# Reordering accumulating products and splitting operand preparation in a 3-stage attention and mixture-of-experts kernel

## The chip, the cores and the metric

One core of one Trainium2 chip runs the whole program. The metric is device time in microseconds of one execution, given as the median of several runs. Before: 1076.45 us, the median of 3 runs (1072.89 to 1079.51).

## The reference

Three stages follow one another, all in float32:

```python
x = attention(rmsnorm(q) * g_q, rmsnorm(k) * g_k, v)    # 4 x 12 heads, 448 x 64
e = argmax(x @ w_gate); gate = softmax(x @ w_gate)[e]    # 1792 tokens, 768 wide
x = gate * (relu(x @ w1[e]) @ w2[e])                     # 8 experts, 768 -> 1024 -> 768
a, b = x @ m_w1, x @ m_w2                                # 768 -> 1024
out = ((a * b) @ m_w3) @ m_wo                            # 1024 -> 1024 -> 768
```

The change touches the end of the expert stage and the stage that computes `a * b`.

## The kernel before, in words

Every float32 operand of a product is held as two float16 parts, an upper one (the value rounded) and a lower one (the rest). ScalarE writes the upper part, VectorE then subtracts it from the value to get the lower one; `split` (L920) does both for weights. `mm3` (L927) makes each product of three matmuls: upper times upper, lower times upper, upper times lower. `m_w3 @ m_wo` is multiplied out early, beside the attention.

**Experts** (`expert`, L972, loop at L1171). Expert r runs 8 hidden blocks (f phase, 144 matmuls) and 6 output blocks (d phase, 144 matmuls) on its tokens, 320 down to 192 of them. After each block `between(r)` (L1149) issues other work: `convert` splits weight blocks of the next expert (6 of `w1`, 8 of `w2`), `stage` (L1072) issues the next weight load into one of four buffers on SP's queue, `ask` and `turn_rows` fetch the next tokens. Also there: at r = 1 one step of `extras` (L791), a table for tokens beyond an expert's capacity, whose rest runs just before expert 3; `overflow` (L1016) then reads its count `nxi` into registers of all engines and branches. At r = 3 to 5, seven steps of `operands(0)` (L1034); at r = 6 and 7, the first calls of `first_weights` (L1138).

**The last products** (`half`, L1248). `a` and `b` are computed by a 2 x 2 block scheme with seven products in place of eight. The activations are cut in two halves of columns, s = 0 (2 x 384) and s = 1 (2 x 512); `operands(s)` forms seven operands of each (B11, B21, B22 and four differences T1 to T4). The weights come in pieces (fp, z, j): output blocks fp = 0 to 3, matrix z = 0 or 1 (`m_w1` or `m_w2`), row blocks j = 0 to 2. A piece is turned from 64-bit to 32-bit floats (`from64`, L204: three VectorE instructions), four sums are formed (L1122 to L1125), and it is split (L1130). `half(fp, s)` runs, for z = 0 and 1, seven products of 9 matmuls each (3 blocks j, 3 matmuls each), in this order, with the PSUM bank and what reads it:

- A11*B11 starts a bank; ScalarE copies it out (`u`, L1290). A12*B21 adds to the same bank, read again (L1294 or L1298).
- S2*T2 starts a bank; VectorE adds it to `u`.
- S3*T3 starts a bank; VectorE makes `t1` from it. A22*T4 adds to the same bank; VectorE makes `x21`.
- S1*T1 starts a bank; VectorE adds it to `t1`. S4*B22 adds to the same bank; VectorE adds it to `u`.

So three of the seven products add to a bank whose first sum was read one instruction earlier. For z = 1 each result is multiplied with that of z = 0 (`finish`, L1278) and split into `ab` by ScalarE and GpSimd (`done`, L1273).

After each product `rest()` (L1268) calls `fill(slot, us)` (L1203): it adds the product's time, less that of its own VectorE read, to a credit (at most 2.5 us) and issues steps from the list `todo` while the credit is positive and the step's slot has come. In `todo` stand the seven steps of `operands(1)`, then sums and splits of the pieces of fp = 1 to 3. Sums run on VectorE for fp = 1, on GpSimd for fp = 2 and 3. `force` (L1211) issues what is still missing before a z begins. After `half(0, 0)` the rest of `operands(1)` is issued in one go (L1342).

Each engine works in the order in which its instructions are written: `flow.pin()` fixes that order for all of them. The last stage (L1364 on) multiplies `ab` by the prepared weights, with 672 matmuls.

Of the kernel before, what the change touches and what calls it, by code (L numbers as in the profile page):

```python
# [8 lines left out]
F32 = mybir.dt.float32  # L9
F16 = mybir.dt.float16  # L10
# [110 lines left out]
def fused_kernel(ctx, tc, q, k, v, g_q, g_k, w_gate, w1, w2, m_w1, m_w2, m_w3, m_wo, out):  # L121
# [831 lines left out]
    def bank(n):  # L953
        return mm_p.tile([P, 512], F32, tag="mm", name="psm")[:, 0:n]
# [79 lines left out]
    def operands(s):  # L1034

        c1, c2 = halves(s)
        b11, b21, b12, b22 = y32[:, 0:3, c1], y32[:, 3:6, c1], y32[:, 0:3, c2], y32[:, 3:6, c2]
        tt = nc.vector.tensor_tensor

        unit = 3 * PC[s][1] / 1000  # L1040

        def put(o, x):
# [3 lines left out]
        put(B11, b11)  # L1046
        yield 1.16 * unit
        put(B21, b21)
        yield 1.16 * unit
        put(B22, b22)  # L1050
        yield 1.16 * unit
# [7 lines left out]
        put(T3, b12)  # L1059
        yield 2.32 * unit  # L1060
        tt(b21, b21, b22, op=ALU.subtract)
        put(T4, b21)
        yield 2.32 * unit
# [47 lines left out]
    def stage_sums(item, home, e):  # L1111
# [8 lines left out]
        y = y.bitcast(F32)  # L1120
# [7 lines left out]
    wst2 = {}  # L1128

    def stage_split(item):  # L1130
        fp, z, j, y = item
        t = w1p.tile([P, 2, DF], F16, tag="w1", name="m2w")[:, :, 0:7 * P]
        split(t, y[:, 0:7].rearrange("p a b -> p (a b)"), 16.0)
        wst2.setdefault((fp, z), []).append(t)

    sums_ = []

    def first_weights():  # L1138
        if staged:
            k = staged[0][1] * 3 + staged[0][2]  # L1140
            sums_.append(stage_sums(staged.pop(0), xtp if k % 2 else ycv, nc.vector))
            stage()
        if len(sums_) > 1 or not staged:
            stage_split(sums_.pop(0))
# [4 lines left out]
    def between(r):  # L1149
        def go(i):  # L1150
# [4 lines left out]
            if r == 1:  # L1155
                next(excess, None)
# [25 lines left out]
    while sums_:  # L1182
        first_weights()
# [16 lines left out]
    todo, credit = [], 0.0  # L1200
    last_operand = None

    def fill(slot, us):  # L1203

        nonlocal credit
        credit = min(credit + us, 2.5)
        while todo and todo[0][0] <= slot and credit > 0:
            credit -= todo[0][1]()
            todo.pop(0)

    def force(key):  # L1211

        while len(wst2.get(key, ())) < 3:
            todo.pop(0)[1]()

    second = operands(1)
    for _ in range(7):
        todo.append((0, lambda: next(second)))
    ends = len(todo)
    pieces = [(fp, z, j) for fp in range(1, SB) for z in range(2) for j in range(3)]  # L1220
    loaded, summed = [], []

    def begin_loads(n=1):
        for _ in range(n):
            if pieces:
                loaded.append(stage_load(*pieces.pop(0), dst))

    def sums_step(e):
        def go():
            summed.append(stage_sums(loaded.pop(0), yst, e))  # L1230
            begin_loads()
            return 2.7 if e is nc.vector else 1.9
        return go

    def split_step():
        stage_split(summed.pop(0))
        return 1.1

    for i, (fp, z, j) in enumerate(pieces):
        gate = 28 * (fp - 1) + 22 * z if z or fp > 1 else 0  # L1240
        todo.append((gate, sums_step(nc.vector if fp == 1 else nc.gpsimd)))
        if i:
            todo.append((gate, split_step))
    todo.append((0, split_step))
    begin_loads(2)
    ab = []

    def half(fp, s):  # L1248
# [34 lines left out]
        later = []  # L1283
        for z in range(2):
            force((fp, z))
            w = wst2[fp, z]
            ps = bank(n)
            product(ps, w, A11, B11, True)
            u = temp("ub" if z else "ua", s)
            nc.scalar.activation(u, ps, AF.Copy, scale=1.0 if z else r)  # L1290
            rest()
            product(ps, w, A12, B21, False)
            if z:
                tt(a[0, 0], ps, a[0, 0], op=ALU.mult)  # L1294
                done(0, 0, a[0, 0])
            else:
                a[0, 0] = temp("a11", s)
                nc.scalar.activation(a[0, 0], ps, AF.Copy, scale=r)  # L1298
# [5 lines left out]
            ps = bank(n)  # L1304
            product(ps, w, S3, T3, True)
            t1 = temp("u3", s)
            add(t1, ps, u, z)
            rest()
            product(ps, w, A22, T4, False)
            x21 = temp("c21", s)  # L1310
            add(x21, ps, u, z)
            outs = [((1, 0), x21), ((1, 1), t1), ((0, 1), u)]

            def end(i):
                k, x = outs[i]
                if not z:
                    a[k] = x
                elif len(ab) == 1:
                    later.append((k, a[k], x))
                else:  # L1320
                    finish(k, a[k], x)

            end(0)
            rest()
            ps = bank(n)
            product(ps, w, S1, T1, True)
            add(t1, ps, t1, z)
            end(1)
            rest()
            product(ps, w, S4, B22, False)  # L1330
            add(u, ps, u, z)
            end(2)
# [6 lines left out]
    ab.append(ab0p.tile([P, 2, NT], F16, name="ab0"))  # L1339
    h = half(0, 0)  # L1340
    next(h)
    for _ in second:  # L1342
        pass
    while todo and todo[0][1].__name__ == "<lambda>":
        todo.pop(0)
# [12 lines left out]
    assert not todo  # L1358
# [42 lines left out]
```

## Time and profile before

| | us |
|---|---|
| median of 3 runs | 1076.45 |
| lowest, highest | 1072.89, 1079.51 |
| the profiled execution, its own time | 1066.05 |
| its span, first to last instruction | 1064.3 |
| attention and routing, to | 375.5 |
| experts, to | 654.5 |
| the products of `half`, to | 947.7 |
| last products and output, to | 1064.3 |

PE is TensorE, DVE VectorE, ACT ScalarE, POOL GpSimd, SP the queue that issues most loads. The times of stages are starts of PE's first matmuls in the profiled execution. In a timeline row the brackets give the idle time of the engine before the group and what ended it.

### The profile page before, as it was taken

The numbers are of one execution on the slowest core, as the hardware profiler recorded it, in microseconds if no ns is written. First come the engines' busy times: TensorE is split into PE (matmuls) and PEld (weight loads), VectorE is DVE, ScalarE is ACT, GpSimd is POOL, SyncE is SP. The second block draws the span as 40 slices with busy tenths as digits, with TensorE's granted clock in tenths as the row PEclk, the third lists the DMA queues.
The fourth block names the chain that finished last, engine by engine and source line by source line (L and its number), as shares of the span: only waits on it lengthen the run. The fifth ranks groups of instructions, "written<-read, shape, count | busy, mean of one in ns | idle before, by whom it ended". The sixth has DMA issues, their size and how long they took to land.

```text
span 1064.3 us, 19475 instructions
## 1 busy us (share of the span) xinstructions
PE 889.7 (84%) x7766; PEld 590.8 (56%) x7766; DVE 647.1 (61%) x959; ACT 478.5 (45%) x738; POOL 309.2 (29%) x317
## 2 busy tenths in 40 slices
PE   0588899999999899997998796757776877899997
PEld 0255566666666477885897795323332433446664
DVE  6898898788988633554656769646746644330000
ACT  4797788888784433453655554221212211110000
POOL 6275667767331251100010100010324322121111
PEclk9898899999999899998998898879899998999999
DMA  7767698875999857873895784102201101011111
GB/s 190 186 134 181 153 200 157 181 153 108 218 213 218 233 157 186 255 221 116 240 280 160 220 247 131 40 0 80 79 20 60 60 21 44 3 72 60 45 60 45
DMA packets 200350, 144.43 MB, mean 136 GB/s; under 512 B 139376, under 2 KB 178832, under 8 KB 200256
## 3 DMA queue, kind: packets, MB, share of 16 engines
q1 hardware_dynamic: 197248, 131.39, 48.0%
q0 software_dynamic: 3008, 11.76, 3.3%
q8 instruction: 62, 1.02, 0.4%
q14 instruction: 32, 0.26, 0.1%
HBM read 103.52 MB, written 14.18 MB: 111 GB/s over the span
## 4 chain that ended last, share of the span: by engine, by line
PE 29%; DVE 11%; DMA 5%; ACT 4%; issue 3%; SPq 1%; POOLq 0%; DVEq 0%; ACTq 0%
PE psm L933 20%; PE pso L1371 10%; DMA st<-in_moe_w_dram 4%; ACT b L1043 1%; DVE m2w L922 1%; DVE y32w L206 1%; DVE u L1266 1%; DVE w1t L922 1%; DVE y32w L207 1%; DVE u L1264 1%; DVE w2t L922 1%; DVE b L1044 1%; DMA xte<-xr 1%; DVE y32w L205 1%; SPq L950 1%
## 5 line engine op out<-in xcount | busy, mean ns | idle before, releaser
L933 PE MATMUL psm<-b,m2w 128*128 128x384 f16 (+1 forms) x1008 | 213.8, 370 | 79.4 <-DVE u L1264 28.0
L933 PEld LDWEIGHTS <-m2w 128*128 128x128 f16 x1008 | 102.1, 102 | 190.7 <-issue 104.9
L933 PEld LDWEIGHTS <-w1t 128*128 128x128 f16 x1152 | 111.6, 100 | 41.5 <-issue 9.3
L933 PE MATMUL psm<-xte,w1t 128*128 128x288 f16 (+6 forms) x1008 | 111.5, 274 | 22.6 <-PEq L1020 7.8
L933 PE MATMUL psm<-ht,w2t 128*128 128x320 f16 (+7 forms) x1152 | 125.4, 270 | 1.9 <-DVE w2t L922 1.9
L933 PEld LDWEIGHTS <-w2t 128*128 128x128 f16 x1152 | 108.8, 98 | 17.2 <-DVE w2t L922 2.9
L1371 PE MATMUL pso<-ww,ab 128*128 128x384 f16 x672 | 109.4, 326 | 0.0
L404 DVE TENSOR_REDUCE nm<-psm 128x2 f32<-128x896 f32 x84 | 88.6, 1084 | 11.5 <-PE psm L402 11.2
L461 PE MATMUL po<-vf,e 128*128 128x65 f32 (+1 forms) x576 | 89.7, 274 | 4.6 <-ACT w L227 4.6
L1371 PEld LDWEIGHTS <-ab 128*128 128x128 f16 x672 | 65.8, 98 | 43.6
L922 DVE SCALAR_TENSOR_TENSOR w1t<-st,w1t 128x1024 f16<-128x1024 f32 x42 | 51.2, 1224 | 56.5 <-ACT w1t L921 54.8
L461 PEld LDWEIGHTS po<-vf,e 128*128 128x128 f32 (+1 forms) x576 | 70.7, 179 | 20.3 <-issue 12.3
L402 PE MATMUL psm<-kt,qt 64*64 64x448 f16 x336 | 47.4, 380 | 37.9 <-DMA qt<-qf 28.2
L723 POOL DMA_INDIRECT xr<-xd,ix x19 | 23.3, 1226 | 191.0 <-DMA ix<-md 120.3
L431 PE MATMUL pss<-qt,kt 64*128 64x448 f16 (+1 forms) x576 | 67.8, 377 | 11.1 <-DVE e L446 10.0
L1375 DVE TENSOR_SCALAR ob<-pso,meta_s 128x384 f32<-128x384 f32 x14 | 8.6, 617 | 99.8 <-PE pso L1371 99.8
L1276 POOL TENSOR_TENSOR ab<-a,ab 128x384 f16<-128x384 f32 (+1 forms) x8 | 8.6, 1078 | 196.0 <-ACT ab L1275 196.0
L464 PE MATMUL po<-v,e 128*128 128x65 f16 (+1 forms) x480 | 63.9, 195 | 1.7 <-DVE lacc L525 1.7
L465 PE MATMUL po<-vl,e 128*128 128x64 f16 (+1 forms) x480 | 63.8, 194 | 0.0
L922 DVE SCALAR_TENSOR_TENSOR w2t<-st,w2t 128x768 f16<-128x768 f32 x56 | 52.9, 955 | 16.7 <-ACT w2t L921 15.6
L466 PE MATMUL po<-v,e 128*128 128x65 f16 (+1 forms) x480 | 63.0, 194 | 0.0
L446 DVE TENSOR_TENSOR e<-pss,e 128x896 f16<-128x896 f32 x48 | 51.6, 1083 | 7.1 <-ACT e L444 6.8
(256 smaller groups left out, 1636.9 us busy)
## 6 DMA issues: line engine op xcount, KB each, us to landing
st<-in_moe_w_dram SPq DMA_DIRECT2D x42, 512.0 KB, 5.4
st<-in_moe_w_dram SPq DMA_DIRECT2D x56, 384.0 KB, 4.1
st<-in_moe_w_dram SPq DMA_DIRECT2D x48, 256.0 KB, 3.3
w<-in_moe_w_dram SPq DMA_DIRECT2D x16, 512.0 KB, 4.9
w<-in_moe_w_out_dram SPq DMA_DIRECT2D x16, 384.0 KB, 3.7
xd<-rx SPq DMA_DIRECT2D x12, 448.0 KB, 4.6
kf<-in_k_dram SPq DMA_DIRECT2D x24, 192.0 KB, 2.9
qf<-in_q_dram SPq DMA_DIRECT2D x24, 192.0 KB, 3.3
```

What stands on the lines that cost most here:

```text
L402: nc.tensor.matmul(ps[h, z, 0:S], lhsT=s["q"][0][h, c:c + 64], rhs=s["k"][0][h, S * j:S * j + S], start=True, stop=True)
L404: nc.vector.tensor_reduce(s["nm"][:, t], ps[:, :, 0:S], axis=AX.X, op=ALU.max, negate=True)
L431: nc.tensor.matmul(ps[o, h, 0:S], lhsT=l, rhs=rt[HD[h], S * j:S * j + S], start=a == 0, stop=a == 3)
L446: nc.vector.tensor_tensor(lo, p, hi, op=ALU.subtract)
L461: nc.tensor.matmul(ov[r, t, :], lhsT=e[0], rhs=vfs[i % 2][:, h, c, 0:D + 1], start=z == 0, stop=z == 3)
L464: nc.tensor.matmul(ov[r, t, :], lhsT=e[0], rhs=vh, start=z == 0, stop=False)
L465: nc.tensor.matmul(ov[r, t, 0:D], lhsT=e[0], rhs=s["vl"][:, h, c, :], start=False, stop=False)
L466: nc.tensor.matmul(ov[r, t, :], lhsT=e[1], rhs=vh, start=False, stop=z == 3)
L723: nc.gpsimd.indirect_dma_start(out=dst, out_offset=None, in_=xd, in_offset=bass.IndirectOffsetOnAxis(ap=ix[0:dst.shape[0], t:t + 1], axis=0))
L922: nc.vector.scalar_tensor_tensor(dst[:, 1], src, scale, dst[:, 0], op0=ALU.mult, op1=ALU.subtract)
L933: nc.tensor.matmul(ps, lhsT=x, rhs=y, start=first and j == 0, stop=last and j == n - 1, **kw)
L1371: nc.tensor.matmul(pp[z], lhsT=ab[f][:, x, ts], rhs=ww[f][:, y, z * 384:(z + 1) * 384], start=f == 0 and x == 0 and y == 0, stop=f == 7 an ...
```

## The change

Three things. In `half` the products are reordered: A11*B11, S2*T2, S3*T3 and S1*T1 each start a bank, then A12*B21, A22*T4 and S4*B22 add to the first, third and fourth of them. `operands` and the making of weight pieces become generators in which ScalarE's upper part is issued one step ahead of VectorE's lower part, with one or two VectorE instructions in a step; `operands(0)` takes 12 steps, `operands(1)` 11. Four of the six pieces of fp = 0 are made between expert blocks (instead of all six before `half(0, 0)`), the other two within `half(0, 0)`, ahead of `operands(1)`; the middle pieces (j = 1) of fp = 1 get their sums on GpSimd. The steps of `extras` run at r = 1 and 2.

```diff
+        def hi(o, x):
             nc.scalar.activation(bt[s][o][:, 0], x, AF.Copy)
+        def lo(o, x):
             tt(bt[s][o][:, 1], x, bt[s][o][:, 0], op=ALU.subtract)
...
-        tt(b12, b12, b11, op=ALU.subtract)
-        put(T1, b12)
-        yield 2.32 * unit
-        tt(b22, b22, b12, op=ALU.subtract)
-        put(T2, b22)
-        yield 2.32 * unit
...
+        hi(T1, b12)
+        lo(B22, b22)
+        yield unit
         tt(b22, b22, b12, op=ALU.subtract)
+        yield unit
+        hi(T2, b22)
+        lo(T1, b12)
+        yield unit
         tt(b12, b22, b11, op=ALU.subtract)
+        yield unit
+        hi(T3, b12)
+        lo(T2, b22)
+        yield unit
         tt(b21, b21, b22, op=ALU.subtract)
+        yield unit
+        hi(T4, b21)
+        lo(T3, b12)
+        yield unit
+        lo(T4, b21)
+        yield unit
...
-    loads = [(r, k) for r in range(1, NE) for k in range(14)] + [(NE, k) for k in range(1, 6)]
-    loads.insert(loads.index((NE - 1, 6)), (NE, 0))
+    loads = [(r, k) for r in range(1, NE) for k in range(14)] + [(NE, k) for k in range(2, 4)]
+    for k in (0, 1):
+        loads.insert(loads.index((NE - 1, 6)), (NE, k))
...
+    def in_parts(n, blocks_, sums):
+
+        b, t = [], []
+        for k in range(n + 1):
+            if k:
+                t.append(stage_upper(b.pop(0)))
+            if k < n:
+                b.append(blocks_(k))
+                c = sums(b[-1])
+                yield k, 1.8 + c
+            if t:
+                stage_lower(t.pop(0))
+                yield k, 1.1
...
+    first_weights = in_parts(4, first_blocks, lambda b: stage_sums(b, nc.vector) and 1.15)
...
-            if r == 1:
+            if r in (1, 2):
                 next(excess, None)
...
-            if i in {LR: (9, 11), LR + 1: (9, 11, 13), LR + 2: (9, 11)}.get(r, ()):
+            if i in {LR: (8, 10, 12), LR + 1: (9, 10, 11, 12, 13), LR + 2: (9, 11, 12, 13)}.get(r, ()):
                 next(early)
-            if r == NE - 2 and i == 13 or r == NE - 1 and i in (8, 10, 12):
-                first_weights()
+            for _ in range({NE - 2: (0, 0, 0, 0, 1, 1), NE - 1: (1,) * 6}[r][i - 8] if i >= 8 and r >= NE - 2 else 0):
+                next(first_weights)
...
+    def steps():
+        second = operands(1)
+        pieces = [(0, 1, 1), (0, 1, 2)] + [(fp, z, j) for fp in range(1, SB) for z in range(2) for j in range(3)]
+        loaded = [stage_load(*x, dst) for x in pieces[:2]]
...
+            own_ = fp == 0 or fp == 1 and j != 1
+            stage_sums(b, nc.vector if own_ else nc.gpsimd)
...
+        for k, c in in_parts(2, blocks_, sums):
+            yield 0, c
+        for c in second:
+            yield 0, c
+        done2.append(True)
+        for k, c in in_parts(len(pieces) - 2, lambda k: blocks_(k + 2), sums):
+            fp, z, j = pieces[min(k + 2, len(pieces) - 1)]
+            yield 28 * (fp - 1) + 22 * z if z or fp > 1 else 0, c
...
+            p1 = bank(n)
+            product(p1, w, A11, B11, True)
             u = temp("ub" if z else "ua", s)
...
+            p4 = bank(n)
+            product(p4, w, S1, T1, True)
+            add(t1, p4, t1, z)
+            end(z, (1, 1), t1)
+            rest()
+            product(p1, w, A12, B21, False)
...
+            product(p3, w, A22, T4, False)
             x21 = temp("c21", s)
-            add(x21, ps, u, z)
...
+            add(x21, p3, u, z)
+            end(z, (1, 0), x21)
             rest()
...
+            product(p4, w, S4, B22, False)
+            add(u, p4, u, z)
+            end(z, (0, 1), u)
             rest()
...
-    for _ in second:
-        pass
-    while todo and todo[0][1].__name__ == "<lambda>":
-        todo.pop(0)
+    while not done2:
+        one()
     ylife.close()
```

## Rows read from the trace of the kernel before

**Rows 1.** Waits of PE, 654 to 948 us: total us, times, longest.
```profile
PE psm L933 <- DVE u L1264: 28.0, 16, 4.7
PE psm L933 <- ACT ua L1290: 27.3, 8, 11.1
PE psm L933 <- DVE u L1266: 14.6, 16, 2.4
PE psm L933 <- ACT ub L1290: 5.2, 8, 0.7
```

**Rows 2.** Windows: length; busy PE, PEld, DVE, ACT, POOL; clock; DMA share, GB/s.
```profile
654.50:709.50 55.00, 28.33 (x138) 14.65 (x136) 36.27 (x46) 16.92 (x19) 2.17 (x3) 0.79 0.06 20
709.50:749.80 40.30, 31.65 (x126) 13.12 (x126) 24.49 (x47) 6.47 (x10) 5.40 (x6) 0.90 0.16 53
749.80:783.80 34.00, 25.05 (x126) 12.94 (x126) 23.74 (x40) 6.84 (x12) 11.43 (x16) 0.90 0.24 78
...
947.70:1064.30 116.60, 109.16 (x672) 65.52 (x670) 10.09 (x16) 8.75 (x15) 15.71 (x16) 0.99 0.14 54
```

**Rows 3.** Timeline of PE in `half(3, 0)` and `half(3, 1)`, without filled-in work.
```profile
896.82 3.08 PE L933 MATMUL psm<-b,m2w 128*128 128x384 f16 x18 [0.65 <-DVE u L1266]
...
904.22 4.55 PE L933 MATMUL psm<-b,m2w 128*128 128x384 f16 x27 [0.58 <-ACT ub L1290]
...
917.52 5.99 PE L933 MATMUL psm<-b,m2w 128*128 128x512 f16 x27 [0.74 <-ACT ua L1290]
...
924.29 4.04 PE L933 MATMUL psm<-b,m2w 128*128 128x512 f16 x18 [0.78 <-DVE u L1266]
```

**Rows 4.** Timeline at the starts of `half(0, 0)` and `half(0, 1)`.
```profile
662.98 0.95 ACT L921 ACTIVATE m2w<-y32x 128x896 f16<-128x896 f32 x1 [2.90 <-DVE y32x L1125]
...
664.36 7.03 PE L933 MATMUL psm<-b,m2w 128*128 128x384 f16 x27 [7.67 <-ACT ua L1290]
...
709.51 8.10 PE L933 MATMUL psm<-b,m2w 128*128 128x512 f16 x27 [11.10 <-ACT ua L1290]
```

**Rows 5.** Timeline on DVE: one piece's sums begin, then a lower part.
```profile
656.17 0.43 DVE L205 TENSOR_SCALAR y32w<-st 128x512 uint32<-128x512 uint32 x1
...
659.02 1.08 DVE L922 SCALAR_TENSOR_TENSOR m2w<-y32x,m2w 128x896 f16<-128x896 f32 x1
```

**Rows 6.** Groups by line, 654 to 948 us: busy us, mean ns, idle before.
```profile
L1044 DVE TENSOR_TENSOR b<-y,b 128x1536 f16<-128x1536 f32 x7 | 12.3, 1758 | 8.8 <-ACT b L1043 8.8
L1266 DVE SCALAR_TENSOR_TENSOR ua<-psm,ua 128x384 f32<-128x384 f32 (+1 forms) x16 | 10.0, 624 | 36.9 <-PE psm L933 36.9
```

**Rows 7.** Timeline of `half(2, 1)`: a VectorE instruction alone, then one beside GpSimd.
```profile
870.02 0.69 DVE L206 SCALAR_TENSOR_TENSOR y32w<-st,y32w 128x512 uint32<-128x512 uint32 x1
...
870.39 1.33 POOL L1276 TENSOR_TENSOR ab<-a,ab 128x512 f16<-128x512 f32 x1 [19.80 <-ACT ab L1275]
870.74 1.53 DVE L207 SCALAR_TENSOR_TENSOR y32w<-st,y32w 128x512 uint32<-128x512 uint32 x1
```

**Rows 8.** Waits of PE in the experts, 375 to 655 us.
```profile
PE psm L933 <- PEq L1020: 7.8, 1, 7.8
PE psm L933 <- ACT w1t L921: 7.2, 3, 3.3
PE psm L933 <- DVE w1t L922: 5.3, 6, 1.0
```

**Rows 9.** Timeline in the experts: `extras`, a lower part, the last expert.
```profile
484.64 0.68 DVE L837 TENSOR_TENSOR xf<-xe,xs 128x512 f32<-128x512 f32 x1
...
487.93 0.15 DVE L844 CAST nxi<-xt 128x1 int32<-128x1 f32 x1
...
562.29 1.36 DVE L1044 TENSOR_TENSOR b<-y,b 128x1152 f16<-128x1152 f32 x1 [1.23 <-ACT b L1043]
...
630.76 0.43 DVE L205 TENSOR_SCALAR y32w<-st 128x512 uint32<-128x512 uint32 x1 [1.36 <-DMA st<-in_moe_w_dram]
...
644.26 10.41 PE L933 MATMUL psm<-ht,w2t 128*128 128x192 f16 x122 [0.55 <-DVE w2t L922]
```

More of the change, by code (lines that the diff above doesn't have):

```diff
@@ L1126, in stage_sums, with stage_upper, stage_lower, first_blocks @@
         return fp, z, j, y
-    wst2 = {}
-    def stage_split(item):
+    def stage_upper(item):
         fp, z, j, y = item
         t = w1p.tile([P, 2, DF], F16, tag="w1", name="m2w")[:, :, 0:7 * P]
-        split(t, y[:, 0:7].rearrange("p a b -> p (a b)"), 16.0)
-        wst2.setdefault((fp, z), []).append(t)
[L1136 to L1144, printed above, removed]
+        y = y[:, 0:7].rearrange("p a b -> p (a b)")
+        nc.scalar.activation(t[:, 0], y, AF.Copy, scale=16.0)
+        return fp, z, t, y
+    wst2 = {}
+    def stage_lower(item):
+        fp, z, t, y = item
+        nc.vector.scalar_tensor_tensor(t[:, 1], y, 16.0, t[:, 0], op0=ALU.mult, op1=ALU.subtract)
+        wst2.setdefault((fp, z), []).append(t)
+    def in_parts(n, blocks_, sums):
[10 more added lines that the diff above has]
+                yield k, 1.1
+    def first_blocks(k):
+        b = stage_blocks(staged.pop(0), xtp if k % 2 else ycv)
+        stage()
+        return b
+    first_weights = in_parts(4, first_blocks, lambda b: stage_sums(b, nc.vector) and 1.15)
     FC = {0: (0, 1, 0, 1, 0, 1, 0, 0), LR: (0, 1, 1, 2, 1, 1, 1, 1)}
@@ L1181, in fused_kernel @@
         pass
-    while sums_:
-        first_weights()
+    for _ in first_weights:
+        pass
     meta_s = const.tile([P, 2 * TP, 3], U32, name="meta_s")
@@ L1198, in temp, with one @@
         return w2p.tile([P, 2, DM], F16, tag="w2", name=name).rearrange("p a b -> p (a b)").bitcast(F32)[:, 0:PC[s][1]]
-    todo, credit = [], 0.0
-    last_operand = None
+    work, gate, credit = None, 0, 0.0
+    def one():
+        nonlocal gate
+        gate, c = next(work, (1000, 0))
+        return c
     def fill(slot, us):
@@ L1206, in fill, with blocks_, sums @@
         credit = min(credit + us, 2.5)
-        while todo and todo[0][0] <= slot and credit > 0:
-            credit -= todo[0][1]()
-            todo.pop(0)
+        while gate <= slot and credit > 0:
+            credit -= one()
     def force(key):
         while len(wst2.get(key, ())) < 3:
[L1214 to L1245, printed above, removed]
+            one()
+    done2 = []
+    def steps():
+        second = operands(1)
+        pieces = [(0, 1, 1), (0, 1, 2)] + [(fp, z, j) for fp in range(1, SB) for z in range(2) for j in range(3)]
+        loaded = [stage_load(*x, dst) for x in pieces[:2]]
+        def blocks_(k):
+            b = stage_blocks(loaded.pop(0), yst)
+            if k + 2 < len(pieces):
+                loaded.append(stage_load(*pieces[k + 2], dst))
+            return b
+        def sums(b):
+            fp, z, j, y = b
+            own_ = fp == 0 or fp == 1 and j != 1
+            stage_sums(b, nc.vector if own_ else nc.gpsimd)
+            return 1.15 if own_ else 0
+        for k, c in in_parts(2, blocks_, sums):
[6 more added lines that the diff above has]
+            yield 28 * (fp - 1) + 22 * z if z or fp > 1 else 0, c
+    ab = []
     ab = []
@@ L1283, in half, with end @@
         later = []
+        def end(z, k, x):
+            if not z:
+                a[k] = x
+            elif len(ab) == 1:
+                later.append((k, a[k], x))
+            else:
+                finish(k, a[k], x)
         for z in range(2):
@@ L1286, in half @@
             w = wst2[fp, z]
-            ps = bank(n)
-            product(ps, w, A11, B11, True)
+            p1 = bank(n)
+            product(p1, w, A11, B11, True)
             u = temp("ub" if z else "ua", s)
[L1290 to L1298, printed above, removed]
+            nc.scalar.activation(u, p1, AF.Copy, scale=1.0 if z else r)
             rest()
@@ L1303, in half @@
             rest()
-            ps = bank(n)
-            product(ps, w, S3, T3, True)
+            p3 = bank(n)
+            product(p3, w, S3, T3, True)
             t1 = temp("u3", s)
-            add(t1, ps, u, z)
+            add(t1, p3, u, z)
             rest()
-            product(ps, w, A22, T4, False)
-            x21 = temp("c21", s)
-            add(x21, ps, u, z)
[L1312 to L1323, printed above, removed]
-            rest()
[L1325 to L1332, printed above, removed]
+            p4 = bank(n)
[4 more added lines that the diff above has]
+            product(p1, w, A12, B21, False)
+            if z:
+                tt(a[0, 0], p1, a[0, 0], op=ALU.mult)
+                done(0, 0, a[0, 0])
+            else:
+                a[0, 0] = temp("a11", s)
+                nc.scalar.activation(a[0, 0], p1, AF.Copy, scale=r)
+            rest()
+            product(p3, w, A22, T4, False)
+            x21 = temp("c21", s)
+            add(x21, p3, u, z)
+            end(z, (1, 0), x21)
+            rest()
+            product(p4, w, S4, B22, False)
+            add(u, p4, u, z)
+            end(z, (0, 1), u)
             rest()
@@ L1339, in fused_kernel @@
     ab.append(ab0p.tile([P, 2, NT], F16, name="ab0"))
+    work = steps()
     h = half(0, 0)
     next(h)
-    for _ in second:
-        pass
-    while todo and todo[0][1].__name__ == "<lambda>":
-        todo.pop(0)
+    while not done2:
+        one()
     ylife.close()
@@ L1357, in fused_kernel @@
                     pass
-    assert not todo
+    assert next(work, None) is None
     prep2.close()
```

35 lines of the change are left out of this document (21 added, 14 removed).

## The prediction

> **What bounds the kernel now.** I read the page's busy shares first (PE 84%, DVE 61%), then the windows by stage, then PE's waits in the stages that the change touches, then the timeline there. The last stage is full (109 of 116.6 us busy at clock 0.99, [rows 2]) and stays as it is. The stage between, 654.5 to 947.7 us, takes 293.2 us. What PE needs for it at full clock follows from [rows 3]: a product of 9 matmuls takes 4.55 - 3.08 = 1.47 us with 384 columns and 5.99 - 4.04 = 1.95 us with 512. There are 56 of each (4 blocks, 2 matrices, 7 products): 82.3 + 109.2 = 191.5 us. The other 101.7 us are waits and slow matmuls. The four rows of [rows 1] add up to 75.1 us: 48 waits, one for each of the three adding products of a z, 16 times over. Where nothing else is queued, such a wait is 0.58 to 0.78 us [rows 3]; 48 of those would be about 33 us. The rest is engine order: the instruction that reads the bank stands behind filled-in work. At 664.36 PE had waited 7.67 us for ScalarE's copy, which stood behind splits that waited for VectorE's sums, and at 709.51 it had waited 11.10 us, behind `operands(1)` [rows 4]. After such waits the matmuls run slow (27 in 8.10 us where 5.99 is the full pace, [rows 3, 4]) and the granted clock of the first three windows is 0.79 to 0.90 [rows 2]. So of the 26.6 us that the waits leave over, most are slow matmuls.
>
> So the stage has two parts. Up to 783.8 us (`half(0, 0)`, `half(0, 1)`, `half(1, 0)`) VectorE is close to full: 36.3 + 24.5 + 23.7 = 84.5 us busy of 129.3 [rows 2], and PE's 20.6 + 27.3 + 20.6 = 68.5 us of work are less than that. From there to 947.7 us (163.9 us) PE's five halves need 123.1 us and VectorE has room.
>
> **Part by part.**
>
> 1. *Reordered products.* No instruction is added. An adding product now comes four products after its bank's start (A12*B21), three (A22*T4) or three (S4*B22), so the read has at least two whole products, 2.9 or 3.9 us, in which to finish, against an empty-queue cost of about 0.7. Four banks per z are open as before, of eight. In the second part this removes all waits that are not longer than the slack. A filled-in burst there is at most the credit of 2.5 us and one step more, some 3 to 4 us of VectorE, and the evictions behind it have two products of time: I leave 3 us for what sticks out. 123.1 + 3 = 126 against 163.9: **-38**. Bounds: 123 (nothing) and 138 (a wait of some 3 us left at each of five bursts), so -41 to -26.
>
> 2. *First part of the stage.* PE no longer waits for ScalarE's copy, so VectorE's chain decides. Its work: the two late pieces of fp = 0 at 659.02 - 656.17 + 1.08 = 3.9 us each [rows 5], 8; what is left of the third and fourth lower parts, 2.5; `operands(1)`, seven lower parts and four differences of the same size at 1.76 [rows 6], 19.5; reads and `finish`, 14 in each half at a mean of 0.62 [rows 6], 26; fp = 1, four pieces at 3.9 and two with sums on GpSimd at 3.0, 22; three of fp = 2, 9. That is 87 with each instruction at its full length. The busy time of before, in which neighbours overlap, was 84.5; it held some 2 us more of sums, which go to GpSimd now. I take 82.5. In front of it comes a new wait: the loads of the two late pieces go into buffers that lie where the earlier ones were, so they can only start at the end of the fourth lower part; 4.5 us from the first product is my value (0 if the memory is free earlier, 8 if all of it waits). Queued behind this wait on VectorE are the reads of S2*T2, S3*T3 and S1*T1; PE runs on until A22*T4, so it loses some 3 us there, and the chain already holds that. Small gaps, 4. Sum 91 against 129.3: **-38**. Bounds: 83 (-46) if it has no gap; 105 (-24) if half of VectorE's idle 44.8 us of before stays.
>
> 3. *Slow matmuls.* They go with the long pauses, and the terms above have them at full pace. `half(0, 1)` still begins after sparse work on PE; I give back 3 us (0 to 10; one such start cost 2.1 before, [rows 3, 4]): **+3**.
>
> 4. *`extras` earlier.* Seven VectorE instructions, 484.64 to 488.08, stood between the last weight of expert 3 and the count that all engines read; PE restarted 4.5 us later, after 7.8 us [rows 8, 9]. The 4.5 us of reading and branching stay. The seven move to expert 2's hidden blocks, beside its `w2` conversions, and I cost them there at nothing; if those conversions are late by them, the gain is gone. **-3.3**, bounds 0 and -7.8.
>
> 5. *`operands(0)` in steps.* In the put of before, VectorE sat 1.23 us at each T for ScalarE [rows 9], with conversions of `w1` behind it. PE's waits for those [rows 8] come to 12.5 us, nearly all at the starts of experts 5 and 6. One step ahead, ScalarE's part is done when VectorE needs it. But loads and ScalarE's conversion also arrive late there, so I take **-5**, bounds 0 and -11.9.
>
> 6. *Weight pieces earlier.* The second piece's load and sums now stand ahead of the eight `w2` conversions of the last expert, on SP's queue (512 KB) and on VectorE (2.85 us, and a wait for that load; the first piece already waited 1.36 us, [rows 9]). Behind them stand the hidden parts and those conversions, and PE needs all eight early in its d phase, where it waited at 644.26 [rows 9]. So PE starts later by about one piece: **+3.2**, bounds 0 and +7. It is paid back in term 2, where the remaining sums no longer stand in front of `half(0, 0)`.
>
> 7. *Sums of two pieces on GpSimd.* It has time. But [rows 7] show a VectorE instruction of two inputs at 1.53 us beside a GpSimd one, against 0.69. The Trainium skill (SBUF — State Buffer, SBUF: two separate sides) calls the shared pair of ports an exclusive lock: the later of the two waits the whole instruction out. The trace agrees with that here: 0.84 us more. By the lock, eight more GpSimd instructions could cost VectorE up to eight such delays, 6.7 us in the first part, in place of the 1.7 us that moving the sums saves; the sum would be 5 us higher. In it they stand at nothing, because most GpSimd rows of the kind fall beside work that is not delayed.
>
> Sum: -38 - 38 + 3 - 3.3 - 5 + 3.2 = **-78**. The profiled execution took 1066.05 us, 1.75 more than its span, so the changed kernel would take 988 of its kind. The runs' median stands 1.0% above that execution; scaled, 988 * 1076.45 / 1066.05 = **997 us**.
>
> **Rivals.** Times are on the median's footing.
>
> *A: bursts still decide.* VectorE and ScalarE stay in order, and a step of sums is 2.85 us in one piece; if reads stand behind steps for longer than two products most of the time, only the short waits go. Then parts one and two end at their bad bounds, -24 and -26, and with 10 us of slow matmuls and the rest as above the gain is 45: 1031 us. For it: at 1.47 us a product, the slack is 2.9 us, hardly more than one step. Against: the credit sets steps to PE's pace.
>
> *B: the experts pay.* If the second piece's load stalls the last expert by its bad bound, +7, the operands give nothing and the `extras` nothing, and the late pieces come 4 us later, the gain is 78 - 3.8 - 3.3 - 5 - 4 = 62: 1014 us. For it: loads bound several waits there. Against: the waits at experts 5 and 6 name VectorE and ScalarE.
>
> *C: the waits change their name.* PE's 48 waits go, but it meets the missing operands and weights instead (lower parts of T2 to T4, of the second z), because VectorE's work is the same. Then the first part gives nothing and the second 26: with the rest 26 - 3 + 5 = 28 less, 1048 us. Against: the first part has 44.8 us in which VectorE is idle.
>
> *D: slower, by the clock.* If PE, paced by VectorE in the first part, is never granted the higher of its two levels (2.4 GHz) and stays at 1.2 through the stage, its 191.5 us become 383, 90 more than the 293 of now; with the experts' 5 gained, 1076 + 85 = 1161 us. It decides from a mean clock under 191.5 / (293 + 5) = 0.64 on. For it: 0.79 in the first window, with PE busy for half of it [rows 2]. Against: `half(3, 0)` and `half(3, 1)` ran at full pace with pauses of 0.6 to 0.8 us after every other product, and the change leaves fewer. The Trainium skill (TensorE: Matmul & The Clock Gate, What's actually happening) says that the throttled state is the default and activity releases it; by that too the second part should be fast.
>
> *E: it does not do what it says.* The order is pinned, so the products will stand as written; only an operand that I have not seen could keep the adding product late. That would be near 1076 - 5 = 1071 us.
>
> **How the numbers follow.** Forecast 0.64, A 0.15, B 0.11, C 0.05, D 0.03, E 0.02. A measurement of this kernel tells about 1% from no change. Faster by over 1%: forecast, A, B and C, 0.95. Within 1%: E, 0.02. Slower: D, 0.03. The forecast's own range is 980 to 1014: below, both parts at their good bounds (-11) and half of what else could come; above, 17 us of the bounds of terms 2, 3, 5 and 6 together. To hold 8 in 10 the range must reach A: 980 to 1033.
>
> **What would show it.** Right: PE's waits name ScalarE's copy of the first bank and VectorE's reads at next to nothing after `half(1, 0)`, and PE is idle for under 30 us in the whole stage; from the start of `half(1, 1)` to the last stage 123 to 130 us; from the first product to there 88 to 95 us, with VectorE busy over 85% of it; PE's pause at the branch before expert 3 near 4.5 us; and a later `w2` wait in the last expert. Wrong: many waits of PE for `m2w` or for the parts of `b`; waits of VectorE for loads at `half(0, 0)` of over 8 us; a granted clock under 0.9 after `half(1, 0)`.

## The result, and the profile after

The changed kernel takes 993.52 us (median of 4 runs, 990.18 to 996.79), the kernel before 1077.98 beside it (4 runs, 1072.89 to 1081.3): 0.922 of the time, 95% interval 0.9168 to 0.9273. The forecast was 997 us.

The profiled execution took 995.48 us with a span of 993.7 us, 70.6 us less than the span of before. Split at the starts of the experts' phases (every 144th matmul) and of the halves (every 126th), the span comes apart like this (us):

| stretch | before | after | difference | forecast |
|---|---|---|---|---|
| up to expert 0 | 375.5 | 374.8 | -0.7 | 0 |
| expert 0 | 40.5 | 50.0 | +9.5 | 0 |
| expert 1 to the first product | 238.5 | 228.8 | -9.7 | -3.3 - 5 + 3.2 = -5.1 |
| products, first three halves | 127.2 | 88.1 | -39.1 | -38 + 3 = -35 |
| products, last five halves | 165.8 | 135.2 | -30.6 | -38 |
| last stage | 116.8 | 116.8 | 0.0 | 0 |

(By count of matmuls `half(1, 1)` of before begins at 781.7 us and the last stage at 947.5; the prediction read 783.8 and 947.7 off the edges of windows.) All products together took 223.4 us; the terms of the forecast make 91 + 126 + 3 = 220.

PE's waits from 645 to 930 us, which answer to [rows 1] (total us, times, longest):

```profile
PE psm L933 <- ACT ua L1343: 10.9, 4, 3.5
PE psm L933 <- DVE u L1310: 4.9, 3, 1.7
PE psm L933 <- ACT b L1043: 3.7, 1, 3.7
PE psm L933 <- DVE b L1046: 2.6, 1, 2.6
PE psm L933 <- DVE m2w L1164: 1.6, 2, 1.3
```

48 waits for readers of a bank, 75.1 us, have become 7, 15.8 us; with the waits for `b` and `m2w` PE is idle for 23.8 us of the stage, 79.4 before. The windows of single halves, with the columns of [rows 2], show where the rest lies:

```profile
653.60:676.00 22.40, 20.79 (x128) 12.12 (x126) 18.82 (x30) 9.41 (x12) 1.51 (x1) 1.00 0.29 95
676.00:717.00 41.00, 30.83 (x129) 12.97 (x127) 39.07 (x54) 13.49 (x16) 8.92 (x13) 0.88 0.20 65
717.00:741.70 24.70, 20.75 (x127) 12.29 (x126) 23.80 (x36) 7.71 (x12) 13.58 (x18) 1.00 0.27 86
741.70:768.90 27.20, 27.20 (x128) 12.31 (x126) 16.79 (x23) 5.41 (x9) 9.09 (x12) 1.00 0.12 39
768.90:797.40 28.50, 23.33 (x128) 13.15 (x127) 24.65 (x34) 7.98 (x13) 17.17 (x25) 0.88 0.28 93
...
824.60:849.70 25.10, 22.25 (x127) 12.78 (x126) 12.83 (x20) 5.18 (x10) 8.20 (x9) 0.93 0.13 47
```

Three readings. In the first three windows VectorE is busy for 18.82 + 39.07 + 23.80 = 81.7 of 88.1 us, so the chain there looks like VectorE's. That its amount of work sets the time is not shown: two kernels below take the same 87.9 us with 75.5 and 74.1 us of it. `half(1, 1)` has no pause at all (27.20 of 27.20 us busy at clock 1.00). `half(2, 0)` and `half(3, 0)` need 20.6 us of PE and take 28.5 and 25.1: what the last five halves lack to the forecast is lost there. The timeline of PE names the places; its first line is the branch before expert 3, the next two lie in `half(0, 1)`, the last three in `half(2, 0)` and `half(3, 0)`:

```profile
496.00 17.55 PE L933 MATMUL psm<-xte,w1t 128*128 128x256 f16 x144 [2.42 <-PEq L1020]
...
681.79 1.01 PE L933 MATMUL psm<-b,m2w 128*128 128x512 f16 x2 [3.68 <-ACT b L1043]
685.41 8.12 PE L933 MATMUL psm<-b,m2w 128*128 128x512 f16 x25 [2.61 <-DVE b L1046]
...
778.47 2.20 PE L933 MATMUL psm<-b,m2w 128*128 128x384 f16 x9 [3.52 <-ACT ua L1343]
782.32 7.90 PE L933 MATMUL psm<-b,m2w 128*128 128x384 f16 x36 [1.65 <-DVE u L1310]
...
833.43 6.88 PE L933 MATMUL psm<-b,m2w 128*128 128x384 f16 x31 [2.85 <-ACT ua L1343]
```

Between the first sum and the one that adds to it stand three products with 384 columns (4.4 us) for the bank that ScalarE copies, two (2.9 us) for the bank at 782.32. That is not enough there, and not for the sake of the bank's own reader alone. The timeline of VectorE shows its delay. It is late already at 768.94, where it reads the sum of A12*B21 of `half(1, 1)`, a product that ended at 765.2; the work filled in last before the end of that half is the turning of a piece (L205 to L207) and two lower parts, and the last reads and the result of the half stand among them.

```profile
768.94 0.68 DVE L1361 TENSOR_TENSOR a<-psm,a 128x512 f32<-128x512 f32 x1
769.54 1.37 DVE L1164 SCALAR_TENSOR_TENSOR m2w<-y32w,m2w 128x896 f16<-128x896 f32 x1
...
772.22 1.38 DVE L205 TENSOR_SCALAR y32w<-st 128x512 uint32<-128x512 uint32 x1
773.63 1.52 DVE L206 SCALAR_TENSOR_TENSOR y32w<-st,y32w 128x512 uint32<-128x512 uint32 x1
775.19 0.69 DVE L207 SCALAR_TENSOR_TENSOR y32w<-st,y32w 128x512 uint32<-128x512 uint32 x1
775.80 0.68 DVE L1308 TENSOR_TENSOR ub<-psm,ub 128x512 f32<-128x512 f32 x1
776.52 0.86 DVE L1323 TENSOR_TENSOR ua<-ua,ub 128x512 f32<-128x512 f32 x1
777.30 1.34 DVE L1164 SCALAR_TENSOR_TENSOR m2w<-y32w,m2w 128x896 f16<-128x896 f32 x1
778.56 0.55 DVE L1310 SCALAR_TENSOR_TENSOR ua<-psm,ua 128x384 f32<-128x384 f32 x1
```

The last result of `half(1, 1)` (L1323) is there only at 777.4, though that half's products ended at 769.1. ScalarE has to take this result to `ab` first and copies the first bank of `half(2, 0)` behind it:

```profile
777.41 0.63 ACT L1319 ACTIVATE ab<-ua 128x512 f16<-128x512 f32 x1 [3.60 <-DVE ua L1323]
777.94 0.47 ACT L1343 ACTIVATE ua<-psm 128x384 f32<-128x384 f32 x1
```

It had waited 3.60 us for it, and PE gets on at 778.47, when the copy is done.

### The profile page after: what moved, and what is told of

Its sections match the earlier page's. It is cut to its first block, busy times and chain, and to the rows that moved or that the text cites. A ratio compares the mean times of both kernels' runs of the same rounds, so it can differ in the third digit from the quotient of the medians.

```text
span 993.7 us, 19480 instructions
## 1 busy us (share of the span) xinstructions
PE 882.1 (89%) x7766; PEld 590.9 (59%) x7766; DVE 646.4 (65%) x951; ACT 477.5 (48%) x738; POOL 316.0 (32%) x325
## 4 chain that ended last, share of the span: by engine, by line
PE 29%; DVE 11%; DMA 5%; issue 3%; ACT 1%; SPq 1%; POOLq 0%; DVEq 0%; ACTq 0%
PE psm L933 18%; PE pso L1412 10%; DMA st<-in_moe_w_dram 5%; DVE y32w L206 1%; DVE y32w L207 1%; DVE m2w L1164 1%; DVE y32w L205 1%; DVE b L1046 1%; DVE w2t L922 1%; DVE w1t L922 1%; DMA xte<-xr 0%; ACT w1t L921 0%; SPq L950 0%; DVE u L1308 0%; DVE ub L1308 0%
## 5 line engine op out<-in xcount | busy, mean ns | idle before, releaser
L933 PE MATMUL psm<-b,m2w 128*128 128x384 f16 (+1 forms) x1008 | 199.8, 362 | 23.8 <-ACT ua L1343 10.9
L933 PE MATMUL psm<-ht,w2t 128*128 128x320 f16 (+7 forms) x1152 | 128.5, 274 | 2.7 <-DVE w2t L922 2.0
L933 PEld LDWEIGHTS <-w2t 128*128 128x128 f16 x1152 | 110.8, 99 | 19.1 <-DVE w2t L922 3.5
L933 PE MATMUL psm<-xte,w1t 128*128 128x288 f16 (+6 forms) x1008 | 108.6, 270 | 12.0 <-DVE w1t L922 4.0
L404 DVE TENSOR_REDUCE nm<-psm 128x2 f32<-128x896 f32 x84 | 88.6, 1083 | 11.3 <-PE psm L402 11.0
L1412 PEld LDWEIGHTS <-ab 128*128 128x128 f16 x672 | 65.6, 98 | 43.7
L464 PEld LDWEIGHTS <-e 128*128 128x128 f16 (+1 forms) x480 | 53.0, 115 | 4.7 <-issue 2.9
```

Source lines behind the costliest of these rows:

```text
L404: nc.vector.tensor_reduce(s["nm"][:, t], ps[:, :, 0:S], axis=AX.X, op=ALU.max, negate=True)
L464: nc.tensor.matmul(ov[r, t, :], lhsT=e[0], rhs=vh, start=z == 0, stop=False)
L933: nc.tensor.matmul(ps, lhsT=x, rhs=y, start=first and j == 0, stop=last and j == n - 1, **kw)
L1412: nc.tensor.matmul(pp[z], lhsT=ab[f][:, x, ts], rhs=ww[f][:, y, z * 384:(z + 1) * 384], start=f == 0 and x == 0 and y == 0, stop=f == 7 an ...
```

## The experiments

The theory after the result: the order of the products gives nearly all of the gain in their stage; the early pieces give the rest, in the first part; what is left at `half(2, 0)` and `half(3, 0)` comes from work filled in just ahead of them. Ten kernels were run; `e3_extras_late`, `e4_sums_on_dve` and `e5_put_early` with one execution each, the others with 4 or 5. Each ratio is against the kernel before, beside it on the same chip.

**The two halves of the change alone.** `e1_order_only` is the kernel before with the new `half`:

```
-            product(ps, w, A12, B21, False)
...
+            p4 = bank(n)
+            product(p4, w, S1, T1, True)
+            add(t1, p4, t1, z)
+            end(z, (1, 1), t1)
+            rest()
+            product(p1, w, A12, B21, False)
```

> The kernel before with the new order of products alone; operands, weight pieces and extras as before. Theory (two causes: the order of products frees the second part, the steps shorten the first): from the start of half(1, 1) on 163.9 us become 126 to 138, as in the changed kernel (135.4), while the first three halves stay above 100 us (88 in the changed kernel, 127 before), since VectorE still makes all of fp = 0 ahead of half(0, 0) and still waits for ScalarE in operands(1); experts as before. Time 1020 to 1040 us. Rival (the steps are what frees VectorE, the order matters little because reads stand behind fills anyway): second part above 150 us, time above 1050.

`e2_steps_only` is the changed kernel with the `half` of before, so with the steps, the early pieces and the sums on GpSimd.

> The changed kernel with the old order of products; all steps, loads and gates as changed. Theory: PE's 48 waits come back, at 0.6 us and more each, second part above 150 us; first three halves 105 to 120 us; experts as in the changed kernel. Time 1035 to 1060 us. Rival (steps matter most): second part under 145 us and time under 1020.

Measured: `e1_order_only` 1014.41 us (1012.94 to 1018.42), 0.9471 [0.9437, 0.9506]; `e2_steps_only` 1049.68 us (1045.83 to 1057.51), 0.9812 [0.9763, 0.9861]. The first three halves took 98.1 and 114.4 us, the last five 135.4 and 163.5. For `e1_order_only` the time and the first three halves lie below what was expected (1020 to 1040 us, above 100 us); the rest came as the theory said. The same view of PE's waits as above, first of `e1_order_only`:

```profile
PE psm L933 <- ACT ua L1299: 13.2, 4, 3.8
PE psm L933 <- DVE m2w L922: 4.5, 3, 2.3
PE psm L933 <- DVE u L1266: 4.4, 3, 2.7
...
PE psm L933 <- DVE u L1264: 1.7, 1, 1.7
```

and of `e2_steps_only`:

```profile
PE psm L933 <- ACT ua L1334: 29.3, 8, 17.6
PE psm L933 <- DVE u L1308: 22.0, 16, 3.2
PE psm L933 <- DVE u L1310: 13.1, 16, 1.5
```

With the old order the waits come 16, 16 and 8 times as in [rows 1], whatever stands ahead of the products; with the new order there are 8 for readers of banks in `e1_order_only` and 7 in the changed kernel. In the last five halves the order does everything (135.4 against 135.2 with both). In the first three, the order alone gives 127.2 - 98.1 = 29 us, more than was expected of it, and the rest of the change the other 10: the steps, the early pieces and the sums on GpSimd, of which only the last were tried alone in this stage (3.0 us, below). The two alone gain 58.5 and 23.2 us, 81.7 together; both at once gain 84.5: within the spread of the runs they add up.

**The steps in the experts.** `e3_extras_late` takes the seven instructions of `extras` back to expert 3 (one execution):

```
-            if r in (1, 2):
+            if r == 1:
```

> The changed kernel with the steps of extras at expert 1 alone, the rest before expert 3 as in the kernel before. Theory: PE's pause at the branch goes from 2.4 us back to 7 to 8, and the time from the start of expert 1 to the first product of half(0, 0) grows by 4 to 6 us. Rival (the pause is made up, since the loads behind the branch set the pace of expert 3): the pause grows, but that time grows by less than 2 us.

PE's pause at the branch is back, and expert 1 to the first product takes 6.7 us longer than after the change (235.5 against 228.8; 225.7 to 231.0 in the eight profiles that have the steps of both `extras` and `operands(0)` as changed), a little more than expected:

```profile
502.21 10.04 PE L933 MATMUL psm<-xte,w1t 128*128 128x256 f16 x75 [7.98 <-PEq L1020]
```

`e5_put_early` is the changed kernel with the `put` of before in `operands(0)`, called where it was called before:

```
-    early, excess = operands(0), extras(ext)
+    early, excess = operands_put(0), extras(ext)
...
-            if i in {LR: (8, 10, 12), LR + 1: (9, 10, 11, 12, 13), LR + 2: (9, 11, 12, 13)}.get(r, ()):
+            if i in {LR: (9, 11), LR + 1: (9, 11, 13), LR + 2: (9, 11)}.get(r, ()):
```

> The changed kernel with operands(0) as before: seven steps in which VectorE waits for ScalarE's upper part. Theory: PE waits more for w1 at the starts of experts 5 and 6 (3.4 and 2.9 us in the changed kernel, 5.9 and 6.0 before), and the time from the start of expert 3 to the first product of half(0, 0), 157.6 us in the changed kernel, grows by 3 to 7 us. Rival (those waits are set by the loads): it grows by less than 1 us.

995.99 us in its one execution, which alone would decide nothing. But the stretch from expert 3 to the first product took 163.1 us, against 157.6 after the change (154.6 to 159.6 in the nine profiles with the new steps, mean 157.1): the steps are worth 5.5 us, 3.5 to 8.5 over that spread. It is the starts of experts 5 and 6 that got longer, from 6.2 us of PE's waits to 10.6, and these two experts together take 68.9 us, against 59.7 to 64.8 in the nine. The timeline of PE has the longest waits:

```profile
561.16 0.27 PE L933 MATMUL psm<-xte,w1t 128*128 128x224 f16 x1 [3.30 <-ACT w1t L921]
...
597.33 0.35 PE L933 MATMUL psm<-xte,w1t 128*128 128x208 f16 x1 [3.30 <-ACT w1t L921]
```

What the earlier pieces cost shows in the last expert: it took 27.1 us before and 28.0 in `e1_order_only`, which make them in the old way, and 30.1 to 32.8 in the ten profiles with early pieces (32.3 after the change), so 2 to 6 us more.

**The two pieces on GpSimd.** `e4_sums_on_dve` gives their sums back to VectorE:

```
-            own_ = fp == 0 or fp == 1 and j != 1
+            own_ = fp <= 1
```

> The changed kernel with the sums of all pieces of fp = 1 on VectorE, as before. By the term of the prediction: half(0, 1) and half(1, 0) together (65.7 us in the changed kernel) change by less than 2 us. Rival, the port lock: without eight GpSimd instructions beside VectorE they get 3 to 7 us shorter. Second rival, VectorE's work alone: 1.7 us or more longer.

995.39 us in its one execution. `half(0, 1)` and `half(1, 0)` took 43.7 + 25.0 = 68.7 us, against 41.0 + 24.7 = 65.7, and 65.7 also in `e3_extras_late` and `e5_put_early`, which have the same code there:

```profile
672.90:716.60 43.70, 31.89 (x127) 13.24 (x126) 40.22 (x61) 12.75 (x15) 4.30 (x5) 0.88 0.16 49
716.60:741.60 25.00, 20.83 (x128) 12.26 (x127) 23.23 (x36) 7.41 (x12) 11.12 (x14) 1.00 0.26 84
```

So the second rival was right: GpSimd's part saves 3.0 us, and a net cost of its standing beside VectorE does not show here. `e10_more_gpsimd`, the fastest kernel below with all sums of fp = 1 on GpSimd, tried the same step further:

> The kernel of e9_quiet_and_gates with the sums of all pieces of fp = 1 on GpSimd. Theory (VectorE's own work bounds half(0, 1) and half(1, 0); two pieces moved that way were worth 3 us): half(0, 1) and half(1, 0) together 2 to 6 us shorter than in e9_quiet_and_gates. Rival (the port lock): GpSimd instructions now stand beside VectorE's through both halves, and their sum is 0 to 4 us longer.

976.51 us (973.52 to 980.93), 0.9143 [0.9095, 0.919], and 65.4 us in these two halves with and without it: no change, so the theory missed. Here the cost does show. Up to the end of `half(1, 1)` the 16 sums moved took 4.6 us off VectorE, but the turning of pieces (L205 to L207) and the lower parts, as many as without it, took 3.0 us longer; VectorE's busy time in the first three halves fell from 75.5 to 74.1 us, and the time did not follow (87.9 us both).

**What is left at the starts of halves.** Three kernels ask what makes the copy of the first bank late. Equal code differs here too: `half(2, 0)` took 28.4 us in the changed kernel and in `e4_sums_on_dve`, 26.6 in `e3_extras_late` and `e5_put_early`; `half(3, 0)` took 25.2 in all four. `e6_gates_late` lets the pieces of z = 0 be made from 14 products later on:

```
-            yield 28 * (fp - 1) + 22 * z if z or fp > 1 else 0, c
+            yield 28 * (fp - 1) + (22 if z else 14) if z or fp > 1 else 0, c
```

> The changed kernel with the pieces of z = 0 of fp = 2 and 3 released 14 slots later, in the 512-column half instead of the 384-column half before it. Theory (VectorE's filled-in work is what PE still waits for): half(1, 0) 24.7 -> 21 to 22.5 us, half(2, 0) 28.4 -> 25 to 27, half(3, 0) unchanged within 1, ratio to the changed kernel 0.994 to 0.997. Rival (ScalarE's copy behind the last result of the half before is what PE waits for): half(2, 0) and half(3, 0) unchanged within 0.5 us, half(1, 0) at most 1 us shorter.

995.12 us (985.86 to 996.34), 0.9256 [0.9191, 0.9322]: no gain, and the theory missed on the ratio, on `half(1, 0)` and on `half(3, 0)`. PE's waits for VectorE's reads fall from 4.9 to 1.4 us, but those for ScalarE's copy stay (10.9 before):

```profile
PE psm L933 <- ACT ua L1343: 11.5, 4, 3.4
...
PE psm L933 <- DVE u L1310: 1.4, 1, 1.4
```

`half(2, 0)` took 26.3 us, inside the spread above. `half(3, 0)` shrank to 23.4 us, with PE busy for 20.6 us at clock 1.00 instead of 22.3 at 0.93. `half(1, 0)` grew by 3.1 to 27.9: PE was busy for 23.6 us in it instead of 20.8, at a mean granted clock of 0.88. A lower part was also held by the gate of the piece after it, and `force` had to issue it, but PE waited only 0.5 us for that.

`e7_quiet_end` fills nothing in behind the last three products of a half with 512 columns:

```
-            fill(slot, us - ev)
+            if s and slot % 14 >= 11:
+                credit = min(credit + us - ev, 2.5)
+            else:
+                fill(slot, us - ev)
```

> The changed kernel with nothing filled in behind the last three products of a 512-column half; the credit is kept for the next half. Theory (the last fills of a half make VectorE late, and with it the first adding product of the next half): PE's waits for ScalarE's ua and VectorE's u at the starts of half(1, 0), half(2, 0) and half(3, 0), 12 us in all, shrink to under 4, half(2, 0) 28.4 -> 22 to 24 us, half(3, 0) 25.2 -> 21 to 22; time 5 to 10 us shorter. Rival (the work only moves to the next half, whose products are shorter): sum of half(1, 0) to half(3, 0) within 2 us of the changed kernel's 157.7.

988.02 us (986.04 to 989.97), 0.9182 [0.9117, 0.9248]. The interval overlaps that of the changed kernel; the stage, 215.8 us against 223.4, tells more. The waits for ScalarE's copy fall from 10.9 to 2.7 us, those for VectorE's reads rise from 4.9 to 6.8, and `half(1, 0)`, `half(2, 0)` and `half(3, 0)` take 22.8, 25.6 and 22.3 us:

```profile
PE psm L933 <- DVE u L1310: 6.8, 5, 3.1
...
PE psm L933 <- ACT ua L1346: 2.7, 1, 2.7
```

So the way was as expected and the size was not reached: at the starts of these three halves 6.3 us of waits are left where under 4 were expected. The work did not only move: `half(1, 0)` to `half(3, 0)` took 125.0 us against 132.7 (157.7 in the expectation is not this sum).

`e8_held_result` leaves the filled-in work and moves only the last result: `finish` of (0, 1) is issued behind the copy of the next half's first bank.

```
+            elif k == (0, 1):
+                held.append((finish, k, a[k], x))
...
+            for f, *x in held:
+                f(*x)
+            held.clear()
```

> The changed kernel with the last result of a half (its VectorE product, ScalarE and GpSimd instructions) issued behind ScalarE's copy of the next half's first product, so that the copy stands behind nothing. Theory (VectorE is late itself): the waits for ScalarE's copy at the starts of halves go, but those for VectorE's u in the third product grow, so half(2, 0) gets 1 to 4 us shorter (28.4) and half(3, 0) 1 to 3 (25.2). Rival (only the copy's place in ScalarE's order costs): both waits go, half(2, 0) 21 to 23 and half(3, 0) 21 to 22.

992.87 us (989.07 to 996.51), 0.9245 [0.9178, 0.9312]. At the starts of `half(1, 0)`, `half(2, 0)` and `half(3, 0)` the copy is no longer late, but PE now waits for VectorE's read in its place, 10.8 us where it was 4.9:

```profile
PE psm L933 <- DVE u L1310: 10.8, 4, 5.9
...
PE psm L933 <- ACT ua L1345: 2.5, 1, 2.5
```

The three starts differ. At `half(2, 0)` PE waits 5.9 us, where it was 3.5 + 1.7: VectorE itself is late there, and the half takes 27.9 us, inside the spread of equal code. At `half(1, 0)` and `half(3, 0)` the waits shrink from 4.0 and 2.9 us to 2.6 and 1.5: there the copy's place behind the last result did cost 1.4 us each, as the rival has it. `half(3, 0)` takes 22.1 us, also because PE's clock stays at 1.00.

`e9_quiet_and_gates` puts the two together: the quiet end, z = 0 pieces due later, and a lower part going by its own piece's gate instead of the next one's.

```
-            yield 28 * (fp - 1) + 22 * z if z or fp > 1 else 0, c
+            fp, z, j = pieces[min(k + 2 if c == 1.1 else max(k + 1, 2), len(pieces) - 1)]
+            yield 28 * (fp - 1) + (22 if z else 14) if z or fp > 1 else 0, c
```

> The kernel of e7_quiet_end with the pieces of z = 0 of fp = 2 and 3 released 14 slots later, as in e6_gates_late, but with the last lower part of the group before them kept at that group's own slot. Theory (VectorE's filled-in work is what is left in half(1, 0), half(2, 0) and half(3, 0), 22.8, 25.6 and 22.3 us in e7_quiet_end; and e6_gates_late lost at half(1, 0) because that lower part was held back): half(1, 0) 21 to 22.5, half(2, 0) 21.5 to 24, stage 211 to 214 us against 216.0. Rival (the slots do not matter once the end of a half is quiet): each within 0.5 us of e7_quiet_end.

975.51 us (974.46 to 977.44), 0.9139 [0.9098, 0.9181]: the lowest of all. As expected, `half(1, 0)` and `half(2, 0)` take 22.4 and 22.1 us and the stage 212.1. The last five halves take 124.2 us, where PE's work is 123.1; the windows of `half(0, 1)`, `half(2, 0)` and `half(3, 0)`:

```profile
669.20:712.20 43.00, 32.95 (x128) 13.53 (x126) 39.52 (x54) 13.50 (x16) 9.99 (x14) 0.84 0.19 62
...
761.80:783.90 22.10, 20.66 (x127) 12.32 (x126) 14.25 (x21) 5.13 (x9) 9.82 (x10) 1.00 0.08 26
...
811.10:831.70 20.60, 20.60 (x128) 12.33 (x127) 10.87 (x18) 5.15 (x10) 7.08 (x6) 1.00 0.17 57
```

The first three halves gained nothing (87.9 us): `half(0, 1)` took 2.0 us more than after the change, with PE busy for 33.0 us instead of 30.8 at a lower clock. PE's wait of 0.6 us for `m2w` at the second z of `half(1, 0)` is the same as in `e7_quiet_end`, so what the lower part's own gate is worth is not shown.

## Why the prediction was right, and where its terms were off

1. *Second part, -38 forecast, -30.6 measured.* The step that failed is "I leave 3 us for what sticks out": 135.2 - 123.1 = 12.1 us stick out, 7.8 in `half(2, 0)` and 4.6 in `half(3, 0)` (the three wide halves ran 0.3 under the 27.3 each that were reckoned). Of the two, 8.0 are PE's waits and 4.4 slow matmuls behind them. The reason given for 3 us, two products of time for each eviction, holds inside a half (27.20 us without a pause). It fails at the start of the narrow halves. There VectorE still has the wide half's last reads, its result and the work filled in between, one behind the other, with some of the instructions stretched beside GpSimd (L205 at 1.38 us against 0.43 in [rows 5]); that the filled-in work is what makes it late is shown by `e7_quiet_end` and `e9_quiet_and_gates`, where 12.1 us become 6.3 and 1.1. Rival A was right on a small scale, in two halves of five.

2. *First part, 91 us forecast (94 with the slow matmuls of term 3), 88.1 measured.* VectorE's work was right: 81.7 us busy, 82.5 said. The step that failed is the new wait in front of it: the 4.5 us for the late pieces' loads did not come. Their sums start right behind the lower part ahead of them:

```profile
655.03 1.09 DVE L1164 SCALAR_TENSOR_TENSOR m2w<-y32x,m2w 128x896 f16<-128x896 f32 x1 [2.87 <-ACT m2w L1157]
656.13 0.43 DVE L205 TENSOR_SCALAR y32w<-st 128x512 uint32<-128x512 uint32 x1
```

VectorE was idle for 6.4 us in all, where 4.5 + 4 had been put; 2.9 of them are the wait for ScalarE's upper part in the first row. On PE the chain shows as waits of 3.7 and 2.6 us at `half(0, 1)` for parts of `b`, which `operands(1)` makes.

3. *Slow matmuls, +3.* PE was busy 199.7 us in the eight halves (the row for `m2w` in the profile page's groups has 199.8), 8.2 over the 191.5 of full pace; before it was 213.8, 22.3 over. The forecast's 3 us for `half(0, 1)` were 3.5 (30.8 against 27.3); the other 4.4 lie in `half(2, 0)` and `half(3, 0)` and came with the waits of term 1. The windows are those with clock 0.88 and 0.93, where PE pauses. The other halves shown are at 1.00, and rival D is out.

4. *`extras`, -3.3.* The step that failed is "The 4.5 us of reading and branching stay". With the count there early PE's pause is 2.42 us, against 7.8 [rows 8]: -5.4. `e3_extras_late` gives 7.98 back.

5. *`operands(0)`, -5.* Worth 5.5 by `e5_put_early`. 6. *Weight pieces, +3.2.* 2 to 6, by the length of the last expert.

7. *Sums on GpSimd, 0.* Worth 3.0 by `e4_sums_on_dve`. The Trainium skill (SBUF — State Buffer, SBUF: two separate sides) calls the shared pair of ports an exclusive lock; the prediction's estimate by that rule was a cost of 5 us. Single instructions of VectorE do take longer beside GpSimd (1.52 us for L206, 0.69 in [rows 7]), so the trace agrees as to the mechanism. For two pieces what was moved off VectorE outweighs it; for four more, in `e10_more_gpsimd`, it does not.

The sum of the terms was -78 for the profiled execution, and -70.6 came. Of the difference, +9.5 is expert 0, which no run shows to hang on the change (below); the rest of the span gave -80.1. That this lies so near to -78 is luck in part: the first part gained 4 us more than forecast and the experts 4.6 more, the second part 7.4 less. So is the forecast of the median. Scaling by 1.0% (the product is 997.6, not 997) added 9.6 us as a proportion, and in the profiled execution 9.5 us came as a pause in one place.

Of the signs that the prediction named, these held: PE idle for under 30 us in the stage (23.8), 88 to 95 us for the first part with VectorE busy over 85% of it (88.1, 93%), and later `w2` waits in the last expert. These did not: 123 to 130 us from `half(1, 1)` on (135.2), next to no waits for the copy and the reads after `half(1, 0)` (8.0 us), and a pause near 4.5 us at the branch (2.4). One of its signs of being wrong came: a granted clock under 0.9 after `half(1, 0)`, in one window, `half(2, 0)` at 0.88.

Of the rivals, B and C are out: the stretch from expert 1 on is shorter, and PE's waits for operands and weight pieces in the products' stage are 3.7 + 2.6 + 1.6 us. E is out by the order that `e1_order_only` tells apart.

## What to carry to other kernels

Where a product adds to a bank that another engine reads in between, put whole products between its first sum and the second: the order alone was worth 5% here. Then look at what is queued on the reading engine at each boundary, because a slack of two or three products is spent at once by work filled in just ahead of it; leaving the last three products before a boundary free, and releasing the next pieces one half later, brought the stage to within 1.1 us of PE's work in its second part. And a wait that names one engine may be another's: when the held result took ScalarE out of the way, the wait at `half(2, 0)` stood at VectorE, as long as before.

## What the runs showed of the hardware that was not expected

PE can pause where nothing in the profile ends the pause. The first phase of expert 0, 144 matmuls, took 19.6 us in the profile of before and 28.9 after the change, with pauses that the timeline puts down to "issue":

```profile
381.05 0.30 PE L933 MATMUL psm<-xt,w1t 128*128 128x320 f16 x1 [0.23 <-issue]
...
382.46 0.30 PE L933 MATMUL psm<-xt,w1t 128*128 128x320 f16 x1 [1.12 <-issue]
...
385.29 0.69 PE L933 MATMUL psm<-xt,w1t 128*128 128x320 f16 x2 [1.80 <-issue]
...
387.42 0.42 PE L933 MATMUL psm<-xt,w1t 128*128 128x320 f16 x1 [1.43 <-issue]
```

It took 26.3 to 28.5 us in the profiles of `e1_order_only` to `e8_held_result` as well, but 21.6 in `e6_gates_late`, and 19.6 in the last two, as in `e9_quiet_and_gates`:

```profile
378.86 19.73 PE L933 MATMUL psm<-xt,w1t 128*128 128x320 f16 x144
```

The kernel before, run beside those last two, had its lowest median too (1066.25 us, against 1072.86 to 1077.98 beside the others). The profiled execution of `e6_gates_late`, with most of the pause missing, took 985.86 us, its other four 994.57 to 996.34. So the pause differs from one execution of a kernel to the next, and how often it comes may go with the occasion or the chip; of the executions without a profile it is not known. Of the 18 us between the medians of the changed kernel and `e9_quiet_and_gates` only about 9 are then the kernel's by the ratios (0.922 and 0.9139, whose intervals just overlap); the products' stage alone is 11.3 us shorter. What causes the pause stays open: no run was made for it.
